# Splitting weights in two steps, separate PSUM banks and other DMA queues in an attention plus GELU feed-forward kernel

## The chip, the core and the metric

The kernel runs on one NeuronCore of one Trainium2 chip, in one launch. Its work is spread over the engines TensorE (PE in the profile; its weight loads are PEld), VectorE (DVE), ScalarE (ACT) and GpSimd (POOL); SyncE (SP) only starts DMAs. Each engine works through its own instructions in the order in which the program lists them, and waits on semaphores for the others. The metric is device time in microseconds (us); lower is better.

## What is computed

Eight batches of twelve heads go through an attention with a sigmoid in place of the softmax, and the result through a feed-forward layer with an exact GELU:

```python
scores = scale * np.matmul(q, k.transpose(0, 1, 3, 2)) - np.log(S)      # q, k, v: (8, 12, 448, 64)
attn = 1.0 / (1.0 + np.exp(-scores))
x = matmul(attn, v).transpose(0, 2, 1, 3).reshape(3584, 768)
h = x @ w_in                                                            # w_in: (768, 2048)
g = 0.5 * h * (1.0 + erf(h / sqrt(2)))
return g @ w_out                                                        # w_out: (2048, 768)
```

The weights come as 64-bit floats, so the kernel first has to decode them to fp32.

## The kernel before, in words

**Attention** takes the first quarter of the time. It walks over 24 units (8 batches x 3 groups of heads), computes scores, sigmoid and the product with v, and stores each unit's result x to a DRAM scratch `scr_x` from GpSimd's queue (`park`, L407). Beside it a `Decoder` (L99) turns chunks of 64-bit weights into fp32 on DVE and ACT and stores them to `scr_f` and `scr_out`.

**The feed-forward part** works on four blocks of two batches each. A product in full fp32 accuracy is made of three fp32r matmuls: every operand is split into a high part (a cast to fp32r, on ACT) and a low part (operand minus high part, on DVE), and `terms` (L473) issues weight-low x data-high, weight-high x data-low, weight-high x data-high, in that order. So a matmul on a tile can start only when ACT and then DVE have been at it.

Block 0 computes the first layer plainly (`ffn1_plain`, L522): 16 weight units, each used for two halves of the columns, 18 matmuls per use, 576 in all. All other layers use Winograd's variant of Strassen's scheme: seven block products in place of eight. `ffn1` (L586) does this for the first layer of blocks 1 to 3, `ffn2` (L630) for the second layer of blocks 0 to 3. Each of these seven stages is 28 weight units of 18 matmuls, 504 matmuls. The order of the products is written out by hand:

- `IN_ORDER` (L64) lists 56 products (p, j) of 9 matmuls, two to a weight unit. They run in chains: 1 then 2; 6 then 7 then 4; 5 then 3. Product p of a chain follows one step behind the one before it (`lag`), and **a chain shares one PSUM bank**: 7 is added on top of 6 in the same bank, after DVE has read the bank for 6 (L610), 4 on top of that, 3 on top of 5 (L616). After product 2 ACT applies the GELU straight from the bank; after 4, 5 and 3 DVE adds a stored sum into a `tmp` tile (L616) and ACT applies the GELU to it.
- `OUT_ORDER` (L71) lists 28 products (p, c), 18 matmuls each, block products in the order 1, 2, 5, 6, 3, 7, 4, four c each. Banks are shared in the same chains; after the fourth c ACT or DVE empties three banks (L658 to L677). Product 2 is added into product 1's banks once ACT has copied them out (L658).

The steps to be followed in the code:

- **Weights** (class `Weights`, L199). Per unit: a DMA on SP's queue into one of three staging tiles `wst` (L226), the high cast on ACT (L236) and the low part on DVE (L237) into one of four `whl` tiles. `get` for unit i first prepares up to unit i+3. Unit i+3 takes over the tile of unit i-1, so its cast waits until PE is through with that unit.
- **Operands of the second layer** (`build`, L512): high cast on ACT (L265), low part on DVE (L266), both issued two units ahead.
- **Operands of the first layer** (`x_load`, `x_sum`, `x_split`, L565 to L584): during `ffn2` of one block the x of the next is loaded (12 DMAs on SP's queue, L262, issued in unit 0), combined on DVE (L574) and split. The splits of block products 1 and 2 are issued in units 26 and 27 (L701 to L704).
- **Block sums of w_in** (`remix`, L707): loads from `scr_f` on SP's queue (L717), four DVE operations (`mix`, L93 to L96), seven or four stores to `scr_in` on GpSimd's queue (L723). j = 0 to 3 are made during `ffn2` of block 0 (units 2, 8, 14, 20, with three DRAM copies each, `recopy`), j = 4 to 7 during `ffn1` of block 1, in the tiles of g (L620).
- **x of the plain stage**: x0 (first half of the columns) is loaded and split at the end of attention (L460 to L468), x1 (second half) at the start of `ffn1_plain` (L522 to L526), six DMAs each on SP's queue.
- **PSUM**: attention has one pool of 3 x 2 banks (`ps_sc`) and one of 2 banks (`ps_av`); the feed-forward part then opens one pool of 8 banks (L744) and rotates through it.

## Time and profile before

| | us |
|---|---|
| device time, median of 3 runs | 1097.01 |
| lowest, highest | 1096.9, 1098.97 |
| the profiled execution's own time | 1101.73 |
| its span, first to last instruction | 1100.0 |
| of it attention, to the first feed-forward matmul | 259.68 |
| PE busy | 1049.5 (95% of the span) |
| DVE, ACT, POOL busy | 782.1, 603.0, 89.8 |
| granted TensorE clock, mean | 0.989 |

A row of the timeline gives start, length, engine, line of the program, operation, output <- inputs, shapes and count; the bracket at its end is the time for which that engine sat idle just before, and what ended the wait. SPq is SyncE starting DMAs. In a row of groups, "388.2, 355" is busy us and mean ns of one. Matmuls overlap: in an undisturbed stretch one starts every 0.19 us though each is listed with 0.35 us, so PE's busy share says less than the time between starts.

### The profile page before, as it was taken

How to read it: one execution, taken by the hardware profiler on the slowest of the kernel's cores; microseconds unless marked ns; L12 is line 12 of the kernel's file. 1: busy time of each engine (PE TensorE's matmuls, PEld its weight loads, DVE VectorE, ACT ScalarE, POOL GpSimd, SP SyncE). 2: the span in 40 equal slices, each digit the busy share in tenths (PEclk: the TensorE clock that was granted, in tenths of full speed). 3: DMA queues.
4: the chain of work that ended last, by engine and by line, in shares of the span. 5: the costliest groups of instructions: out<-in, count | busy, mean ns of one | idle time of the engine just before them, and what ended most of it. 6: DMA issues, size and time to landing. Idle time of an engine off the chain costs nothing.

```text
span 1100.0 us, 15452 instructions
## 1 busy us (share of the span) xinstructions
PE 1049.5 (95%) x5930; PEld 910.4 (83%) x5930; DVE 782.1 (71%) x989; ACT 603.0 (55%) x805; POOL 89.8 (8%) x142
## 2 busy tenths in 40 slices
PE   9999999997999999797998999999899999998998
PEld 5555555445999999797997899999799999988998
DVE  3777777774787688876666699566569975666795
ACT  5878877765345555354345554544455455446542
POOL 0111111002122123102000000000000000000000
PEclk9999999999999999899999999999999999999999
DMA  8999999887578777777335545433265453333442
GB/s 264 314 308 289 308 298 283 245 255 263 165 246 271 236 273 237 235 235 264 109 100 159 161 123 162 144 113 117 86 204 141 146 159 113 115 101 102 142 132 86
DMA packets 95706, 211.79 MB, mean 193 GB/s; under 512 B 9616, under 2 KB 46864, under 8 KB 95632
## 3 DMA queue, kind: packets, MB, share of 16 engines
q1 hardware_dynamic: 84560, 171.24, 51.2%
q0 software_dynamic: 10912, 39.33, 9.8%
q8 instruction: 47, 0.77, 0.3%
q10 hardware_dynamic: 160, 0.23, 0.1%
q14 instruction: 27, 0.22, 0.1%
HBM read 162.79 MB, written 50.33 MB: 194 GB/s over the span
## 4 chain that ended last, share of the span: by engine, by line
PE 75%; DVE 8%; DMA 7%; ACT 5%; issue 4%; SPq 1%; DVEq 0%; ACTq 0%
PE pf L478 53%; PE pav L386 9%; PE sc L348 8%; DVE whl L237 2%; PE sc_t L365 2%; ACT whl L236 2%; DVE tmp L616 2%; DMA wst<-scr_out 2%; PE pav L399 2%; DMA g<-scr_f 1%; DMA xl<-scr_x 1%; ACT g L504 1%; DMA wst<-scr_in 1%; DMA a<-scr_f 1%; DMA x<-scr_x 1%
## 5 line engine op out<-in xcount | busy, mean ns | idle before, releaser
L478 PE MATMUL pf<-op,whl 128*128 128x448 f32 x2016 | 388.2, 355 | 11.5 <-DVE op L266 6.8
L478 PEld LDWEIGHTS pf<-op,whl 128*128 128x128 f32 x2016 | 382.8, 190 | 16.3 <-DVE op L266 8.2
L478 PE MATMUL pf<-xh_p,whl 128*128 128x448 f32 x1008 | 280.3, 357 | 25.9 <-DVE tmp L616 16.0
L237 DVE TENSOR_TENSOR whl<-wst,whl 128x768 fp32r<-128x768 f32 x212 | 202.1, 954 | 133.6 <-ACT whl L236 133.5
L236 ACT CAST whl<-wst 128x768 fp32r<-128x768 f32 x212 | 175.8, 830 | 205.3 <-PE pf L478 166.7
L478 PEld LDWEIGHTS pf<-xh_p,whl 128*128 128x128 f32 x1008 | 192.1, 191 | 32.7 <-DVE tmp L616 18.2
L478 PE MATMUL pf<-xl_p,whl 128*128 128x448 f32 x504 | 178.9, 355 | 0.0
L331 ACT ACTIVATE a<-sc 128x896 f32<-128x896 f32 x144 | 121.7, 920 | 52.7 <-PE sc L348 52.7
L266 DVE TENSOR_TENSOR op<-g,op 128x896 fp32r<-128x896 f32 x112 | 121.2, 1084 | 9.1 <-ACT op L265 9.1
L386 PE MATMUL pav<-a,v 128*64 128x448 f32 x576 | 119.1, 548 | 0.0
L478 PE MATMUL pf<-xh,whl 128*128 128x448 f32 x384 | 105.9, 357 | 5.9 <-ACT xh L265 5.0
L265 ACT CAST op<-g 128x896 fp32r<-128x896 f32 x112 | 104.6, 935 | 2.2 <-PE pf L478 2.2
L504 ACT ACTIVATE g<-tmp 128x448 f32<-128x448 f32 x72 | 43.7, 621 | 108.9 <-DVE tmp L616 108.9
L478 PEld LDWEIGHTS pf<-xl_p,whl 128*128 128x128 f32 x504 | 96.1, 191 | 0.3
L386 PEld LDWEIGHTS pav<-a,v 128*64 128x64 f32 x576 | 37.0, 136 | 68.0 <-issue 63.6
L478 PEld LDWEIGHTS pf<-xh,whl 128*128 128x128 f32 x384 | 73.6, 192 | 7.3 <-ACT xh L265 5.3
L412 DVE COPY x<-pav 128x448 f32<-128x448 f32 x48 | 29.8, 623 | 62.6 <-PE pav L386 39.6
L478 PE MATMUL pf<-xl,whl 128*128 128x448 f32 x192 | 68.6, 357 | 1.0 <-DVE xl L266 0.8
L348 PE MATMUL sc<-lo,hi 64*128 64x448 f32 x282 | 56.9, 393 | 1.0 <-ACT a L331 1.0
L348 PEld LDWEIGHTS sc<-lo,hi 64*128 64x128 f32 x282 | 26.9, 186 | 36.7 <-ACT me L134 14.8
L131 ACT ACTIVATE me<-me 128x512 f32<-128x512 int32 (+1 forms) x40 | 29.2, 729 | 47.9 <-DVE me L120 47.9
L323 DVE TENSOR_TENSOR lo<-qk,hi 128x896 fp32r<-128x896 f32 x47 | 51.2, 1089 | 1.5 <-ACT hi L320 0.4
(76 smaller groups left out, 940.8 us busy)
## 6 DMA issues: line engine op xcount, KB each, us to landing
wst<-scr_out SPq DMA_DIRECT2D x112, 384.0 KB, 3.2
wst<-scr_in SPq DMA_DIRECT2D x84, 384.0 KB, 3.1
v<-v_dram SPq DMA_DIRECT2D x24, 512.0 KB, 5.6
raw<-w_in_dram SPq DMA_DIRECT2D x16, 768.0 KB, 7.8
raw<-w_out_dram SPq DMA_DIRECT2D x24, 512.0 KB, 5.3
scr_x<-x POOLq DMA_DIRECT2D x24, 448.0 KB, 7.1
out_dram<-tmp SPq DMA_DIRECT2D x48, 224.0 KB, 2.1
qk<-q_dram SPq DMA_DIRECT2D x23, 448.0 KB, 5.3
```

The source lines that it names most:

```text
L131: nc.scalar.activation(e.bitcast(F32), e.bitcast(I32), AF.Relu, bias=1151.0 * 2**23, scale=-8.0)
L236: nc.scalar.copy(hl[:, 0], t)
L237: nc.vector.tensor_tensor(hl[:, 1], t, hl[:, 0], op=ALU.subtract)
L265: nc.scalar.copy(hi, src)
L266: nc.vector.tensor_tensor(lo, src, hi, op=ALU.subtract)
L323: nc.vector.tensor_tensor(lo, raw, hi, op=ALU.subtract)
L331: nc.scalar.activation(to, sc, AF.Sigmoid, bias=NEG_LOG_S, scale=SCALE)
L348: nc.tensor.matmul(sc[:, j], ks[rows(j), 1, keys], braid(qs[rows(j), 0]) if braided else qs[rows(j), 0], start=n == 0, stop=n == last,)
L386: nc.tensor.matmul(pav[rows(j)], vals[u][:, p, j, c], a[:, j], start=p == 0 and c == 0, stop=p == 1 and c == FULL - 1,)
L412: nc.vector.tensor_copy(xs[u][:, p], bank(u, p))
L478: nc.tensor.matmul(bank, a, braid(m), **flags)
L504: nc.scalar.activation(straight(dst), unbraid(src), AF.Gelu)
```

## The change

- **Weights**: `prepare_to` becomes `high_to` (ACT cast) and `low_to` (DVE subtraction). `get` issues the casts up to unit i+3 but the subtractions only up to unit i+2. The staging tile is reloaded after the subtraction.
- **Second-layer operands**: `build` becomes `op_high` (two units ahead) and `op_low` (one unit ahead). First-layer operands: `x_split` becomes `x_high` and `x_low`, issued at separate products.
- **GELU and copies** of `ffn1`, and the difference of two g tiles, are put in a list `later` and issued at the start of the next product (`flush`).
- **Orders**: chains (1, 2) and (5, 3) run with lag 2; `OUT_ORDER` becomes 1, 5, 2, 6, 3, 7, 4.
- **Banks**: products 6, 7 and 4 each take banks of their own, and DVE adds the sums (7 onto g12, 4 onto g22). Products 2 and 3 stay on the banks of 1 and 5 (`CHAINED`).
- **Queues**: all loads of x and the loads of `remix` move from SP's to GpSimd's queue; an x tile takes two DMAs instead of three. `remix` becomes `mix_load` and `mix_store`, four units apart in `ffn2` and several products apart in `ffn1`. The x loads of the next block are issued in unit 1, their sums in units 16, 18, 24 and 25.
- **PSUM**: pools of 6 and 2 banks, taken in turn by the tile's number modulo 8.
- **x1 of the plain stage** is allocated and loaded before the g tiles. `LATE` goes from 18 to 17: one high cast of attention moves from ACT to DVE.

The core of the diff (lines that only rename or reflow are left out):

```diff
+        (p, s - lag * n)
+        for chain, lag in (((1, 2), 2), ((6, 7, 4), 1), ((5, 3), 2))
...
-    OUT_ORDER = [(p, c) for p in (1, 2, 5, 6, 3, 7, 4) for c in range(KF // 2)]
+    OUT_ORDER = [(p, c) for p in (1, 5, 2, 6, 3, 7, 4) for c in range(KF // 2)]
+    CHAINED = {2: 1, 3: 5}
...
-        def prepare_to(self, n):
+        def high_to(self, n):
             while self.ready < min(n, len(self.units)):
                 i = self.ready
+                self.low_to(i + 1 - WST)
                 self.load_to(i + 1)
...
                 nc.scalar.copy(hl[:, 0], t)
+                self.split[i] = hl, t
+                self.ready += 1
+
+        def low_to(self, n):
+            while self.low < min(n, len(self.units)):
+                hl, t = self.split[self.low]
                 nc.vector.tensor_tensor(hl[:, 1], t, hl[:, 0], op=ALU.subtract)
-                self.split[i] = hl
-                self.ready += 1
-                self.load_to(i + WST)
+                self.low += 1
+                self.load_to(self.low + WST)
 
         def get(self, ready=None):
             i = self.taken
-            self.prepare_to(ready or i + WHL)
+            self.high_to(ready or i + WHL)
+            self.low_to(max(i + 1, self.ready - 1))
...
-        for c in range(KC):
-            nc.sync.dma_start(dst[:, c], src[:, c, :, k])
+        for a in range(2):
+            nc.gpsimd.dma_start(dst[:, :, a], src[:, :, a])
...
             if u == total - 1:
                 for hi, lo in x0:
                     split(hi, lo, lo.bitcast(F32))
-                W.prepare_to(2)
+                W.high_to(2)
+                W.low_to(1)
             if u == total:
                 nc.scalar.activation(one, one, AF.Gelu)
-                W.prepare_to(WHL)
+                W.low_to(2)
+                W.high_to(WHL)
...
+            n = count["bank"]
+            count["bank"] += 1
+            pool = banks[n % 8 >= 6]
...
+                ph = held[CHAINED[p], j] if p in CHAINED else bank()
...
                 if p == 1:
-                    nc.scalar.copy(g21, ph)
+                    later.append(lambda g21=g21, ph=ph: nc.scalar.copy(g21, ph))
                 elif p == 2:
-                    gelu(g11, ph)
+                    later.append(lambda g11=g11, ph=ph: gelu(g11, ph))
                 elif p == 6:
-                    nc.vector.tensor_tensor(g12, ph, g21, op=add)
+                    combine(g12, ph, g21, add)
                 elif p == 7:
-                    nc.vector.tensor_tensor(g22, ph, g21, op=add)
+                    combine(g22, ph, g12, add)
...
+                    def close(p=p, r=r, h=h, dst=dst, t1=g[0, 1][c], g11=g[0, 0][c]):
+                        gelu(dst, h)
+                        if p == 3 and r == 1:
+                            later.append(lambda: combine(t1, t1, g11))
+                    later.append(close)
+                at = p, j
+                if b == 1 and at in ((1, 3), (1, 4), (1, 7), (2, 6)):
+                    jm = 4 + ((1, 3), (1, 4), (1, 7), (2, 6)).index(at)
+                    mix_store(jm)
+                    if jm < 6:
+                        mix_load(jm + 2, g)
+                highs = {(1, 2): 6, (1, 5): 7, (1, 7): 4, (6, 3): 5, (7, 7): 3}
+                lows = {(1, 3): 6, (1, 6): 7, (2, 6): 4, (6, 4): 5, (4, 7): 3}
...
             for n, (p, c) in enumerate(OUT_ORDER):
                 hl = W.get()
-                build(b, g, n + 2)
+                op_high(b, g, n + 2)
+                op_low(n + 1)
+                flush()
...
-                if b == 0 and n % 6 == 2 and n // 6 < KF // 2:
-                    remix(n // 6)
-                    recopy(n // 6 + KF // 2)
+                if b == 0:
+                    if n % 6 == 0 and n // 6 < KF // 2:
+                        mix_load(n // 6)
+                        recopy(n // 6 + KF // 2)
+                    if n % 6 == 4 and n // 6 < KF // 2:
+                        mix_store(n // 6)
...
                     if (p, c) == (4, 2):
-                        x_split(nxt, b + 1, 1)
+                        x_high(nxt, b + 1, 1)
                     if (p, c) == (4, 3):
-                        x_split(nxt, b + 1, 2)
+                        x_low(nxt, 1)
+                        x_high(nxt, b + 1, 2)
...
-    ps_f = ctx.enter_context(psum("ps_f", 8))
-    feed_forward(ps_f)
+    banks = [ctx.enter_context(psum(f"ps_f{n}", n)) for n in (6, 2)]
+    feed_forward(banks)
```

In the new `ffn2` the lines shown last stand behind the loop over the three banks of the product, as the old ones did. `x_low(xs, 2)` is issued at product 0 of the next `ffn1`.

More of the change, by code (lines that the diff above doesn't have):

```diff
@@ L206, in __init__ @@
             self.staged, self.split = {}, {}
-            self.loaded = self.ready = self.taken = 0
+            self.loaded = self.ready = self.low = self.taken = 0
         def source(self, i):
@@ L478, in terms, with feed_forward, flush @@
             nc.tensor.matmul(bank, a, braid(m), **flags)
-    def feed_forward(ps_f):
-        ff = late
+    def feed_forward(banks):
         sub, add = ALU.subtract, ALU.add
-        count = [0]
+        count = {"bank": 0, "tmp": 0}
+        later = []
         def bank():
-            count[0] += 1
-            return ps_f.tile([P, 512], F32, tag="pf", name=f"pf{count[0]}")[:, :S]
+            n = count["bank"]
+            count["bank"] += 1
+            pool = banks[n % 8 >= 6]
+            return pool.tile([P, 512], F32, tag="pf", name=f"pf{n}")[:, :S]
         def tmp():
-            count[0] += 1
-            return ff.tile([P, S], F32, tag="tmp", name=f"tmp{count[0]}", bufs=4)
+            count["tmp"] += 1
+            return late.tile([P, S], F32, tag="tmp", name=f"tmp{count['tmp']}", bufs=4)
+        def flush():
+            now = later[:]
+            later.clear()
+            for work in now:
+                work()
         def slots(b):
@@ L550, in ffn1_plain @@
                 if f == 0:
-                    dec.pool = ff
+                    dec.pool = late
                     dec.flush()
@@ L592, in ffn1 @@
                     hl = W.get()
-                key = chain_of[p], j
-                first = p in (1, 6, 5)
-                if first:
-                    banks[key] = bank()
-                ph = banks[key]
-                hi, lo = ops[p]
+                flush()
+                if n == 0:
+                    x_low(xs, 2)
+                ph = held[CHAINED[p], j] if p in CHAINED else bank()
+                held[p, j] = ph
+                hi, lo = xs[p]
                 for cc in range(KC):
@@ L637, in ffn2 @@
             p1, p5, u2 = (x_tile(f"xt{n}", f"y{b}_{n}").bitcast(F32) for n in range(3))
-            chains = {1: "a", 2: "a", 5: "c", 3: "c", 6: "b", 7: "b", 4: "b"}
-            banks = {}
-            nxt, x = {}, {}
+            held, nxt, x = {}, {}, {}
             for n, (p, c) in enumerate(OUT_ORDER):
                 hl = W.get()
-                build(b, g, n + 2)
-                if c == 0 and p in (1, 5, 6):
-                    banks[chains[p]] = [bank() for _ in range(KE)]
-                bs = banks[chains[p]]
-                op = built.pop(n)
+                op_high(b, g, n + 2)
+                op_low(n + 1)
+                flush()
+                if c == 0:
+                    fresh = p not in CHAINED
+                    held[p] = [bank() for _ in range(KE)] if fresh else held[CHAINED[p]]
+                op = ops.pop(n)[0]
                 for e in range(KE):
+                    ph = held[p][e]
                     for f in range(2):
@@ L652, in ffn2 @@
                         o = op[:, 0, f * S : f * S + S], op[:, 1, f * S : f * S + S]
-                        first = p in (1, 5, 6) and c == 0 and f == 0
-                        last = c == KF // 2 - 1 and f == 1
-                        terms(bs[e], w, o, first, last, True)
+                        ends = fresh and c == 0 and f == 0, c == KF // 2 - 1 and f == 1
+                        terms(ph, w, o, *ends, True)
                     if c == KF // 2 - 1:
                         if p == 1:
-                            nc.scalar.copy(p1[:, e], bs[e])
+                            nc.scalar.copy(p1[:, e], ph)
@@ L659, in ffn2 @@
                         elif p == 5:
[L660 removed]
+                            nc.scalar.copy(p5[:, e], ph)
                         elif p == 6:
[L662 to L666 removed]
+                            combine(u2[:, e], ph, p1[:, e], add)
@@ L713, in remix, with mix_store @@
                 a = sb.tile([P, 4 * QUAD], F32, tag="wd", name=f"a{j}", bufs=2)
-                t = ff.tile([P, 4 * QUAD], F32, tag="s", name=f"sin{j}", bufs=1)
+                t = late.tile([P, 4 * QUAD], F32, tag="s", name=f"sin{j}", bufs=1)
                 tiles = [x[:, i * WU : i * WU + WU] for x in (a, t) for i in range(2)]
             for i in range(2):
-                nc.sync.dma_start(tiles[i], scr_f[i * KF + j])
-            quads = [t[:, i * OP : i * OP + OP] for t in tiles for i in range(2)]
+                nc.gpsimd.dma_start(tiles[i], scr_f[i * KF + j])
+            mixes[j] = [t[:, i * OP : i * OP + OP] for t in tiles for i in range(2)]
+        def mix_store(j):
+            quads = mixes.pop(j)
             parts = mix(quads[:4], quads[4:])
             for p, part in parts.items():
-                if not (g and p in (1, 2, 4)):
+                if j < KF // 2 or p not in (1, 2, 4):
                     n = IN_ORDER.index((p, j))
```

210 lines of the change are left out of this document (105 added, 105 removed).

## The prediction

> **What bounds the kernel now.** I read the page first, then the stretches of the feed-forward part by stage, then what PE waited for, then the timeline around each wait. The page's first line gives the span, and the view of stretches the eight stages (first the plain first layer of block 0, then second and first layers in turn):
>
> ```profile
> span 1100.0 us, 15452 instructions
> ...
> 259.68:377.43 117.75, 111.82 (x577) 110.12 (x577) 83.20 (x130) 49.37 (x82) 31.08 (x43) 0.97 0.73 237
> 377.43:482.70 105.27, 98.46 (x506) 96.51 (x504) 88.05 (x102) 53.04 (x67) 21.32 (x40) 0.97 0.75 248
> 482.70:593.95 111.25, 98.83 (x506) 95.92 (x506) 68.24 (x93) 49.92 (x73) 8.54 (x16) 0.98 0.50 162
> 593.95:694.34 100.39, 97.59 (x506) 96.29 (x505) 82.93 (x90) 52.84 (x68) 0.00 (x0) 0.98 0.52 159
> 694.34:799.23 104.89, 98.14 (x505) 95.95 (x504) 62.03 (x78) 50.62 (x73) 0.00 (x0) 0.98 0.38 112
> 799.23:896.86 97.63, 95.90 (x505) 94.93 (x505) 81.55 (x89) 52.60 (x67) 0.00 (x0) 1.00 0.54 163
> 896.86:1000.31 103.45, 96.68 (x506) 94.78 (x506) 60.56 (x77) 50.30 (x73) 0.00 (x0) 1.00 0.37 114
> 1000.31:1096.24 95.93, 95.79 (x505) 94.83 (x503) 73.28 (x82) 48.22 (x63) 0.00 (x0) 1.00 0.41 119
> ```
>
> The columns are: stretch, length, busy time (and count) of PE, PEld, DVE, ACT and POOL, granted clock, DMA share, GB/s. The last seven stages do the same 504 matmuls, yet take from 95.93 to 111.25 us. The last one has next to no idle time, so 95.93 is the floor of such a stage (3.43 per unit of 18 matmuls, 0.19 per matmul), and 576/504 x 95.93 = 109.6 that of the plain one. Over the floor are, in order, 8.1, 9.3, 15.3, 4.5, 9.0, 1.7, 7.5 and 0: 55.4 us. TensorE's stream is the bound, and these are holes in it. What ended the holes:
>
> ```profile
> PE pf L478 <- DVE tmp L616: 16.0, 12, 3.2
> PE pf L478 <- DVE op L266: 6.8, 4, 4.9
> PE pf L478 <- DVE g L610: 6.1, 3, 3.2
> PE pf L478 <- ACT xh L265: 5.0, 1, 5.0
> PE pf L478 <- ACT y L658: 4.3, 2, 2.7
> PE pf L478 <- DVE whl L237: 3.7, 1, 3.7
> ...
> PE pf L478 <- DVE x L412: 1.0, 1, 1.0
> ...
> DVE whl L237 <- ACT whl L236: 133.5, 107, 5.1
> ```
>
> PE's waits make 42.9 us; the rest of the 55.4 is mostly matmuls that run at half rate after a long hole (listed with 0.74 us below). The last row is behind many of them: DVE, in order, stands 133.5 us idle before weight subtractions whose cast ACT has not done, with its other work queued behind.
>
> **Where each hole comes from.** From the timeline:
>
> ```profile
> 458.24 0.56 DVE L93 TENSOR_TENSOR sin<-a 128x384 f32<-128x384 f32 x1 [3.72 <-DMA a<-scr_f]
> 463.73 0.74 PE L478 MATMUL pf<-op,whl 128*128 128x448 f32 x1 [4.94 <-DVE op L266]
> 500.30 0.56 DVE L93 TENSOR_TENSOR g<-g 128x384 f32<-128x384 f32 x1 [4.19 <-DMA g<-scr_f]
> 795.28 0.62 DVE L616 TENSOR_TENSOR tmp<-pf,g 128x448 f32<-128x448 f32 x1
> 795.96 0.74 PE L478 MATMUL pf<-xh_p,whl 128*128 128x448 f32 x1 [3.23 <-DVE tmp L616]
> 799.76 6.60 SPq L262 DMA_DIRECT2D x<-scr_x  x12
> 812.46 0.83 ACT L236 CAST whl<-wst 128x768 fp32r<-128x768 f32 x1 [4.49 <-DMA wst<-scr_out]
> 814.61 1.59 PE L478 MATMUL pf<-op,whl 128*128 128x448 f32 x7 [1.59 <-ACT y L658]
> ```
>
> Second layer of block 0: DVE waits for a block load that has just been started, and the operand splits stand behind it. The change starts that load four units (13.7 us) ahead and on another queue. First layer of block 1: the same with loads into g (500.30), and weight loads behind them on SP. First layers of blocks 1 to 3: PE may not add the next product into a shared bank until DVE has read it (795.28, 795.96); DVE is late because it waits for a GELU in ACT's queue. The change gives 6, 7 and 4 banks of their own, leaves four products between 5 and 3 and runs the GELU a product later, so none of these reads is near PE's path. Second layers of blocks 1 and 2: twelve x loads occupy SP for 6.6 us, the next weight unit comes late (812.46), and product 2 waits for ACT to empty product 1's banks (814.61). With x on GpSimd's queue and all four units of product 5 in between, both go. So I take these holes away and ask what is late next.
>
> **What is late next: the block edge.** In the new order the low part of x for product 1 is issued in unit 27 behind the three additions that empty product 4's banks. Before, it was issued a unit earlier, and only product 2's stood there:
>
> ```profile
> 482.70 0.35 PE L478 MATMUL pf<-xh_p,whl 128*128 128x448 f32 x1
> ...
> 482.90 0.62 DVE L670 TENSOR_TENSOR tmp<-pf,y 128x448 f32<-128x448 f32 x1 [0.51 <-PE pf L478]
> 483.44 1.55 DVE L266 TENSOR_TENSOR xl_p<-x,xh_p 128x1344 fp32r<-128x1344 f32 x1
> ```
>
> The last addition can start only 0.2 us after the stage's last matmul, the subtraction 0.54 later, and it takes 1.55: ready 2.3 us into the new stage. The second matmul of the stage needs it and would start at 0.19. New hole: 2.1, taken as 2.2, at the start of each of three first layers.
>
> **What is late next: after product 6.** The operand's low part now has a lead of one unit, not two. DVE operations follow each other at these distances, with the longer ones beside them:
>
> ```profile
> 438.49 1.08 DVE L684 TENSOR_TENSOR g<-g,g 128x896 f32<-128x896 f32 x1
> 439.49 0.95 DVE L237 TENSOR_TENSOR whl<-wst,whl 128x768 fp32r<-128x768 f32 x1
> 440.36 1.08 DVE L266 TENSOR_TENSOR op<-g,op 128x896 fp32r<-128x896 f32 x1
> ...
> 406.94 1.56 DVE L574 TENSOR_TENSOR x<-x,x 128x1344 f32<-128x1344 f32 x1
> ...
> L93 DVE TENSOR_TENSOR sin<-a 128x384 f32<-128x384 f32 x4 | 2.2, 560 | 8.5 <-DMA a<-scr_f 8.5
> ```
>
> An ordinary unit with a g difference takes DVE 1.00 + 0.87 + 1.00 = 2.9 of 3.43: it can run ahead. The end of product 6 ties it to PE: last addition at 0.20, +0.54, g difference +1.00, weight +0.87, operand +1.08 = 3.7 us after the product's end, needed at 3.43: a hole of 0.3 in each second layer. In block 0, the same unit (16) then holds a block mix (4 x 0.56 = 2.2) and an x sum (1.5), before the next weight (0.87) and operand (1.08): 3.6 + 2.2 + 1.5 + 0.87 + 1.08 = 9.3, needed at 0.3 + 2 x 3.43 = 7.2: 2.1 more. So 2.5 there. Elsewhere the same walk ends in time (after product 7, six additions of 0.55: 3.3 against 3.43).
>
> **The start.** The first feed-forward matmul waits for DVE's copy out of the last attention bank, and x1 is late:
>
> ```profile
> 252.00:260.00 8.00, 7.01 (x40) 2.34 (x37) 6.83 (x8) 6.56 (x8) 0.89 (x2) 1.00 0.31 105
> 260.00:268.00 8.00, 8.00 (x44) 7.99 (x43) 3.85 (x6) 1.92 (x3) 6.15 (x9) 1.00 1.00 329
> ...
> 259.68 0.43 PE L478 MATMUL pf<-xh,whl 128*128 128x448 f32 x1 [0.99 <-DVE x L412]
> ...
> 266.15 11.26 DMA xl<-scr_x
> ...
> 275.09 0.74 PE L478 MATMUL pf<-xh,whl 128*128 128x448 f32 x1 [4.96 <-ACT xh L265]
> ...
> 277.51 1.31 ACT L265 CAST xh<-xl 128x1344 fp32r<-128x1344 f32 x1 [2.48 <-DMA xl<-scr_x]
> ...
> L168 POOL DMA_DIRECT2D scr_out<-s x24 | 17.3, 753 | 57.0 <-DVE s L93 52.5 <-DVE s L96 1.9 <-PE pf L478 1.7
> ```
>
> With a pool of its own the last two banks of attention no longer hold up the first matmul: -1.0. Bounds: if the x0 loads, which now stand behind an x store on GpSimd's queue, came late, the first matmul could be up to 2 us later than before; the DMA share of 0.31 in the stretch before says that the backlog is gone by then, so I take the gain. x1: four starts of 0.75 from 260.5 on, ahead of the `scr_out` stores, which contended with them. Ahead or beside them lie the last x store (448 KB) and two weight units (768 KB); with x1's 1344 KB that is 2.6 MB, at 329 GB/s 8.0 us: landed near 268.5, cast (1.31) and subtraction (1.55) done by 271.4. PE needs this half at 258.7 + 3 x 3.43 + 9 x 0.19 = 270.7. A hole of 0.7, taken as 1.5; bounds 0 (loads alone on the queue) and the present 8.1.
>
> [...]
>
> **Sum.** Over the floor after the change, by stage: 1.5, 2.5, 2.5 (2.2 and 0.3 for block loads), 0.3, 2.2, 0.3, 2.2, 0.3 = 11.8 against 55.4; with the first gap 43.6 + 1.0 = 44.6 us less. The 48 starts that move to GpSimd (24 for the later x, 8 for x0 and x1, 16 for the blocks; 0.75 each, 36 us) lie on an engine with 0 to 31 us of work per stage. A block load there waits until the stores of the mix before have left its tile, and DRAM copies and, in unit 0, the x loads queue behind it; their first users come four units later or more, so I cost that at 0.3 in the first layer of block 1 alone. The one cast that moves from ACT to DVE in attention (`LATE`) I take at nothing, bounds 1 us either way. The profiled execution took 1101.7, so 1057.1 of its kind; it lies 4.7 above the median of the three timed runs, and from that median, 1097.0, I get 1052.4. No hole at all would be 1097.0 - 56.4 = 1040.6.
>
> **Rivals.** First: the data come late all the same. Speaks for it that DMA moves 329 GB/s at a share of 1.00 at the start and 0.75 in block 0; against it, that weight loads no longer stand behind other loads on SP and have about two units to land. Price: the plain stage keeps 8.1 and the first layer of block 1 its 15.3: 1052.4 + 6.6 + 12.8 = 1071.8.
>
> Second: GpSimd is held up by DVE. If it could start DMAs only while DVE is idle, 0.75 becomes 0.75 / (1 - 83.20/117.75) = 2.6 and x1 lands 7.3 later: 1059.7. The later x loads have 15 units, 51 us, before their first use and would hide it.
>
> Third, slower than before: DVE becomes the bound of the second layers because the operand's low part has one unit less of lead. If every unit waited as long for a cast as DVE's weight subtractions do now (133.5 / 107 = 1.25 us), then with 82.93 / 28 = 2.96 us of work it takes 4.21 against 3.43: 0.78 x 112 units = 87 us, 3.4 of which I have already, 1136 in all. It turns the sign from 0.4 us per unit on, that is a wait of 0.87. Against it: each of these subtractions follows its cast by a whole unit in the new order.
>
> Fourth: the banks bring nothing. Tile number modulo 8 over pools of 6 and 2 is the same rotation as one pool of 8, so except for the first gap that part does nothing; if the other moves only shifted the holes, no change. Fifth: the block edge costs nothing (the subtraction runs earlier than I read): 6.6 less, 1045.8.
>
> **How the numbers follow.** My forecast 0.62, the fifth case 0.11, the first rival 0.15, the second 0.06, the third 0.04, no change 0.02. Faster by over 0.2% (2.2 us, about what a measurement of this kernel can tell from no change): 0.94; within: 0.02; slower: 0.04. The range goes from 1044, which holds the fifth case, to 1068, which takes in the second rival and a partial first one; the full first, the third and no change stay out.
>
> **What would show it.** Right: the seven stages of 504 matmuls lie between 96 and 99 us; PE no longer waits for L616, L610 or L658's counterparts; DVE's waits for the weight cast all but vanish from 133.5; the second matmul of each first layer of blocks 1 to 3 waits about 2 us for a low part of x; one hole near unit 17 of block 0's second layer. Wrong: first matmul later than 259.7, x1 landing after 271, a hole in most units of a second layer (third rival), or the first layer of block 1 still above 105 us.

## The result, and the profile after

The changed kernel takes 1058.37 us (median, 1056.78 to 1059.09), the kernel before 1097.49 in the runs beside it (1096.9 to 1098.97): a ratio of 0.964, 95% interval 0.9623 to 0.9656. The forecast was 1052.4 with a range of 1044 to 1068: the sign is right, the range holds the time, and the median lies 6.0 us above the forecast.

Two lines of the page after the change (the profiled execution's own time is 1057.68):

```profile
span 1055.8 us, 15495 instructions
...
PE 1038.8 (98%) x5930; PEld 907.9 (86%) x5930; DVE 785.4 (74%) x990; ACT 605.4 (57%) x804; POOL 122.8 (12%) x190
```

DVE and ACT are as busy as before (782.1 and 603.0); their work was only moved. POOL has 33.0 us more: the 48 DMA starts that came over from SP, 0.54 to 0.78 each.

The view of stretches after the change, in the same eight stages and with the same columns as before:

```profile
259.18:372.97 113.79, 111.28 (x576) 110.25 (x577) 85.00 (x133) 51.49 (x85) 41.58 (x59) 0.99 0.80 260
372.97:470.54 97.57, 95.91 (x505) 94.92 (x505) 84.93 (x100) 51.67 (x67) 26.39 (x49) 1.00 0.78 265
470.54:568.14 97.60, 95.61 (x505) 95.17 (x505) 71.51 (x96) 52.58 (x75) 16.76 (x28) 1.00 0.62 198
568.14:663.78 95.64, 95.64 (x505) 95.07 (x505) 80.73 (x88) 52.21 (x66) 0.00 (x0) 1.00 0.49 141
663.78:761.38 97.60, 95.61 (x505) 95.17 (x505) 63.85 (x79) 51.58 (x74) 6.06 (x8) 1.00 0.48 146
761.38:857.02 95.64, 95.64 (x505) 95.06 (x505) 80.74 (x88) 52.32 (x66) 0.00 (x0) 1.00 0.48 141
857.02:956.31 99.29, 97.30 (x506) 96.54 (x506) 63.85 (x79) 51.78 (x74) 0.00 (x0) 0.98 0.38 116
956.31:1052.11 95.80, 95.80 (x505) 94.91 (x503) 73.41 (x82) 47.49 (x61) 0.00 (x0) 1.00 0.42 122
```

The seven stages of 504 matmuls, which took 95.93 to 111.25 us, now take 95.64 to 99.29. Stage for stage, the time over the floor of 95.93 (109.6 in the plain stage) as forecast and as found:

| stage | before | forecast | after |
|---|---|---|---|
| plain, block 0 | 8.1 | 1.5 | 4.2 |
| second layer, block 0 | 9.3 | 2.5 | 1.6 |
| first layer, block 1 | 15.3 | 2.5 | 1.7 |
| second layer, block 1 | 4.5 | 0.3 | -0.3 |
| first layer, block 2 | 9.0 | 2.2 | 1.7 |
| second layer, block 2 | 1.7 | 0.3 | -0.3 |
| first layer, block 3 | 7.5 | 2.2 | 3.4 |
| second layer, block 3 | 0 | 0.3 | -0.1 |
| sum | 55.4 | 11.8 | 11.8 |

(The last sum is of unrounded figures; the stages after add up to 792.93.)

What PE waited for in the feed-forward part, where there had been 42.9 us of waits, and DVE's wait for the cast of the weights (133.5 before), from the view of waits. In each row: waiting engine, tile and line, what it waited for, us in all, times, longest:

```profile
PE pf L488 <- DVE xl_p L525: 6.0, 3, 2.0
PE pf L488 <- DVE op L525: 1.7, 1, 1.7
...
PE pf L488 <- ACT xh L273: 1.4, 1, 1.4
PE pf L488 <- DVE xl L274: 1.1, 1, 1.1
...
DVE whl L245 <- ACT whl L238: 64.7, 58, 5.9
```

The old rows (`tmp`, `g` and `y`, the reads of shared banks) are gone. Five rows are left in this part. Four were named ahead: the block edge (`xl_p`) three times, unit 17 to 18 of block 0 once (`op`), and x1, cast and low part (`xh`, `xl`). The fifth, 0.3 for the first unit's weights (`whl`), is told at the start below. The block edge in the timeline of the changed kernel:

```profile
469.47 1.90 DVE L525 TENSOR_TENSOR tmp<-pf,y 128x448 f32<-128x448 f32 x3
...
470.54 0.35 PE L488 MATMUL pf<-xh_p,whl 128*128 128x448 f32 x1
471.29 1.55 DVE L525 TENSOR_TENSOR xl_p<-x,xh_p 128x1344 fp32r<-128x1344 f32 x1
...
472.89 0.46 PE L488 MATMUL pf<-xl_p,whl 128*128 128x448 f32 x1 [1.99 <-DVE xl_p L525]
```

Three additions into `tmp`, then the subtraction (`xl_p`) 0.75 after the stage's first matmul, 1.55 long; the second matmul starts 2.35 after the first in place of 0.19. That is 2.16 lost, against 2.2 forecast.

The start in the same timeline. At 244.69 the x0 loads are started behind an x store on POOL's queue, and both casts of x0 wait for them:

```profile
243.97 0.72 POOL L423 DMA_DIRECT2D scr_x<-x  x1 [9.55 <-DVE x L420]
244.69 3.17 POOL L270 DMA_DIRECT2D xl<-scr_x  x4
...
253.42 1.31 ACT L273 CAST xh<-xl 128x1344 fp32r<-128x1344 f32 x1 [0.79 <-DMA xl<-scr_x]
...
255.36 1.31 ACT L273 CAST xh<-xl 128x1344 fp32r<-128x1344 f32 x1 [0.63 <-DMA xl<-scr_x]
...
256.37 2.48 PE L394 MATMUL pav<-a,v 128*64 128x448 f32 x12
...
259.18 0.46 PE L488 MATMUL pf<-xh,whl 128*128 128x448 f32 x1 [0.34 <-DVE whl L245]
...
261.37 3.04 POOL L270 DMA_DIRECT2D xl<-scr_x  x4
...
271.23 1.31 ACT L273 CAST xh<-xl 128x1344 fp32r<-128x1344 f32 x1 [0.25 <-DMA xl<-scr_x]
```

The wait for the last attention bank is gone (before: 0.99, `DVE x L412`), but the weights of the first unit, which DVE splits behind x0, are 0.34 late. Of x1, started at 261.37, the last half is there only at about 271.2 (its cast, at 271.23, has just waited 0.25 for it).

### The profile page after: what moved, and what is told of

Read it like the earlier page. It is cut to its first block, busy times and chain, and to the rows that moved or that the text cites. A ratio compares the mean times of both kernels' runs of the same rounds, so it can differ in the third digit from the quotient of the medians.

```text
span 1055.8 us, 15495 instructions
## 1 busy us (share of the span) xinstructions
PE 1038.8 (98%) x5930; PEld 907.9 (86%) x5930; DVE 785.4 (74%) x990; ACT 605.4 (57%) x804; POOL 122.8 (12%) x190
## 3 DMA queue, kind: packets, MB, share of 16 engines
q0 software_dynamic: 15264, 56.64, 15.3%
## 4 chain that ended last, share of the span: by engine, by line
PE 93%; DVE 2%; DMA 2%; issue 2%; ACT 1%; POOL 0%; DVEq 0%; POOLq 0%; ACTq 0%
PE pf L488 71%; PE pav L394 10%; PE sc L356 8%; PE sc_t L373 2%; PE pav L407 2%; DMA wst<-scr_out 1%; DMA xl<-scr_x 1%; DVE xl_p L525 0%; DMA qk<-k_dram 0%; DVE op L525 0%; POOL xl L270 0%; DVE g L525 0%; DVE whl L245 0%; DVE wd L146 0%; ACT a L339 0%
## 5 line engine op out<-in xcount | busy, mean ns | idle before, releaser
L488 PE MATMUL pf<-op,whl 128*128 128x448 f32 x2016 | 383.5, 353 | 1.7 <-DVE op L525 1.7
L488 PE MATMUL pf<-xh_p,whl 128*128 128x448 f32 x1008 | 274.7, 354 | 0.0
L245 DVE TENSOR_TENSOR whl<-wst,whl 128x768 fp32r<-128x768 f32 x212 | 201.9, 953 | 64.8 <-ACT whl L238 64.7
L525 DVE TENSOR_TENSOR g<-g,g 128x896 f32<-128x896 f32 x64 | 69.3, 1083 | 0.0
L525 DVE TENSOR_TENSOR tmp<-pf,g 128x448 f32<-128x448 f32 x72 | 44.7, 624 | 27.4 <-PE pf L488 25.6
L522 ACT ACTIVATE g<-tmp 128x448 f32<-128x448 f32 x72 | 45.2, 627 | 33.4 <-DVE tmp L525 33.3
L525 DVE TENSOR_TENSOR g<-pf,g 128x448 f32<-128x448 f32 x48 | 29.9, 624 | 37.5 <-PE pf L488 36.4
```

The source lines that it names most:

```text
L245: nc.vector.tensor_tensor(hl[:, 1], t, hl[:, 0], op=ALU.subtract)
L488: nc.tensor.matmul(bank, a, braid(m), **flags)
L522: nc.scalar.activation(straight(dst), unbraid(src), AF.Gelu)
L525: nc.vector.tensor_tensor(out, a, b, op=op)
```

## The experiments

Line numbers in the rows are those of each experiment's own kernel. Three theories. **Causes apart** is the prediction's: each hole has its own cause, and what removes it is one named part. **Casts**: DVE standing in front of weight subtractions is the one cause; the weights part does nearly everything. **Overlap**: a hole needs two late things, so that parts don't add up.

The kernel before is not steady: beside the runs below its median is 1097.5 (parts undone), 1101.1 (parts alone) and 1098.3 (holes that are left), with single executions from 1094.58 to 1103.81. So differences between these groups are known to some 4 us only, and the stages of a profile say more than the totals.

### One part of the changed kernel undone

**Weights** (the low part follows its cast at once again):

```diff
                 self.split[i] = hl, t
                 self.ready += 1
+                self.low_to(self.ready)
```

> The changed kernel, but with the low part of each weight unit issued right behind its high cast again. Three theories. 'Causes apart' (the prediction's): every hole has a cause of its own; here only block 0's second layer, where DVE has block mixes to catch up with, loses some: 1059 to 1063, DVE's idle time before weight subtractions back from 65 to 120 us or more. 'Casts': the one cause of nearly all holes is that DVE stands behind casts that ACT hasn't done; then this undoing brings most of them back: 1078 or more. 'Overlap': a hole needs two things to be late at once, so that undoing any one part costs little: 1058 to 1061.

1075.39 us (1074.44 to 1078.17), ratio 0.9802 (0.9785 to 0.9819): 17.0 more than the changed kernel. From the view of waits:

```profile
PE pf L489 <- DVE op L526: 14.9, 13, 3.2
PE pf L489 <- DVE xl_p L526: 7.6, 3, 3.6
...
DVE whl L246 <- ACT whl L238: 155.3, 148, 5.8
```

The second layer of block 0 has 11.1 of it (97.57 to 108.62), no other stage more than 3.3. DVE stands behind casts 155.3 us again, and what is late on its queue is the operand's low part, which in the new order is issued only one unit ahead. So the split of the weights is what makes the short lead of the operands affordable. The time lies in none of the three ranges expected, nearest to that of "casts"; but the first layers of blocks 2 and 3 stay at 97.60 and 99.28, which "casts" does not explain.

**Queues** (x and block loads back on SP's queue):

```diff
-            nc.gpsimd.dma_start(dst[:, :, a], src[:, :, a])
+            nc.sync.dma_start(dst[:, :, a], src[:, :, a])
...
-                nc.gpsimd.dma_start(tiles[i], scr_f[i * KF + j])
+                nc.sync.dma_start(tiles[i], scr_f[i * KF + j])
```

> The changed kernel, but with the loads of x and of the weight blocks on SyncE's queue again. 'Causes apart': the holes that followed from weight loads standing behind other loads come back at the start (about 4 us), in the second layer of block 0 and the first of block 1 (3 to 6 us each), and 1 or 2 us in the second layers of blocks 1 and 2: 1066 to 1074. 'Casts': at most 3 us more, 1061. 'Overlap': 3 to 8 us more, most of it at the start: 1061 to 1066.

1062.91 us (1062.51 to 1063.96), ratio 0.9685 (0.9671 to 0.97): 4.5 more. The plain stage is longer by 5.3, 119.06 against 113.79; PE's wait for x1's cast grows from 1.4 to 5.3 us. Block loads, x of the later blocks and weights share SP's queue here and no other stage is longer by more than 1.7 (block 2's first layer, where the clock is at 0.50 for 3.4 us behind the block edge). The time lies in the range of "overlap". With `remix` split in two, loads and mix units apart, the queue of the block loads does not matter here.

**Banks** (7 and 4 back in the bank of 6, in both layers, with their sums; the chains 1, 2 and 5, 3 back to a lag of one):

```diff
-        for chain, lag in (((1, 2), 2), ((6, 7, 4), 1), ((5, 3), 2))
+        for chain, lag in (((1, 2), 1), ((6, 7, 4), 1), ((5, 3), 1))
...
-    CHAINED = {2: 1, 3: 5}
+    CHAINED = {2: 1, 3: 5, 7: 6, 4: 7}
```

> The changed kernel, but with block products 6, 7 and 4 in one bank again and a lag of one step in all chains (the sums that DVE adds go back with it). 'Causes apart': the holes of the first layers of blocks 1 to 3 at shared banks come back, 5 to 7 us in each: 1073 to 1079. 'Casts': at most 1061, since DVE now reads the banks in time. 'Overlap': 1 or 2 us in each first layer: 1061 to 1065.

1060.36 us (1059.01 to 1063.03), ratio 0.9664 (0.9647 to 0.9681): 2.0 more, in first layers (100.93, 99.24, 99.24 us); PE waits for the copy of g on ACT three times, 2.6 us in all. Of block 1's 100.93, 1.7 are half-rate matmuls (the clock is at 0.50 from 472.0 to 475.4). "Causes apart" expected 1073 to 1079 and misses by far; "casts" had at most 1061, "overlap" 1061 to 1065.

**GELU** (the list `later` runs at once):

```diff
-        later = []
+        class Now(list):
+            def append(self, work):
+                work()
+
+        later = Now()
```

> The changed kernel, but with the GELU, the copies and the g differences of the first layers issued at once and not at the next product. 'Causes apart': DVE waits for a GELU before each g difference again, but with four products between 5 and 3 that reaches PE only at the end of the chain: 2 to 8 us more, 1060 to 1066. 'Casts' and 'overlap': no more than 2 us, 1058 to 1060.

1058.85 us (1056.37 to 1061.14), ratio 0.9654 (0.9638 to 0.967): 0.5 more, no difference that these runs can show. The second layers of blocks 1 to 3 take 1.35 more each, so the part does something, about 4 us in the profiled execution. There it is made up elsewhere: the start is 1.7 earlier, the plain stage 2.07 shorter (111.72), and block 3's first layer is at 97.60 like the other two, for the clock stays at 1.00 behind its edge. "Causes apart" had expected a loss in the first layers; there is none.

The four add up to 24.0 us, the whole change is worth 39.1. That alone says little, since the four are not the whole change: the order of the second layer's products, the pools of PSUM, `remix` in two steps and the later operand low parts stay in all of them, and no run undoes these. What each part brings alone decides.

### One part alone on the kernel before

**Weights** alone, the split of the change's `high_to` and `low_to` without the rest:

```diff
-            self.prepare_to(ready or i + WHL)
+            self.high_to(ready or i + WHL)
+            self.low_to(max(i + 1, self.ready - 1))
```

> The kernel before, with one part of the change alone: weight units' low parts issued a unit behind their casts. 'Casts': with the one cause gone most of the 39 us are gained, 1062 to 1077. 'Causes apart': 8 to 15 less than before, 1082 to 1089, since shared banks, block loads on SyncE's queue and product 1's copy stay. 'Overlap': each part alone gains more than undoing it costs; for this one, whose undoing cost 17 us: 20 or more, up to 1077.

1128.93 us (1126.37 to 1130.66) against 1101.12 beside it (1094.58 to 1103.81): ratio 1.0253 (1.0209 to 1.0298), 27.8 **slower**. All three theories expected a gain. "Casts" as the one cause falls: DVE's wait for casts of weights goes from 133.5 to 9.6 us, and the kernel loses. ACT's waits say where:

```profile
ACT whl L237 <- DMA wst<-scr_out: 82.3, 23, 10.0
ACT whl L237 <- DMA wst<-scr_in: 33.3, 5, 9.8
```

In the kernel before these two were 17.5 and 10.1. The staging tile is free only after the low part, and the low part comes a unit later; the next weight load starts later by as much. Where x and block loads stand on the same queue, it is late. First layers of blocks 2 and 3, where nothing else is loaded, gain: 97.22 and 97.23 in place of 104.89 and 103.45. The shared queue and three tiles are not enough for the loss, though: the changed kernel with its loads back on SP's queue has both, and there ACT waits 25.3 us for `wst<-scr_out`, not 82.3. Which of the other parts spares it is not shown.

**The same with a fourth staging tile:**

```diff
-WHL, WST = 4, 3
+WHL, WST = 4, 4
```

> The weights part alone on the kernel before, as in the run that came out 27.8 us slower, with a fourth staging tile. If that loss is lost lead (the tile is freed by the low part, which now comes a unit later, so a weight load starts 3.4 us later and more often stands behind x or block loads on SP's queue), a fourth tile gives the lead back: second layers of blocks 0 to 2 back to 98 to 107 us, first layer of block 1 to 111 or less, ACT's waits for the weight load from 82 + 33 us to under 35, total 1070 to 1090 against 1097 to 1101 for the kernel before. If it is DVE (low parts of weights in the way of its other work), it stays near 1125 to 1129.

1103.64 us (1099.08 to 1107.88), ratio 1.0043 (1.0024 to 1.0063): it lies 5.3 above the kernel before where the run without the tile lay 27.8 above, so lost lead was most of that. ACT's waits for weight loads fall from 82.3 and 33.3 to 11.6 (the row of `scr_in` is gone), but DVE has another one:

```profile
ACT whl L237 <- DMA wst<-scr_out: 11.6, 3, 4.9
...
DVE g L93 <- DMA g<-scr_f: 29.4, 4, 8.8
```

The stretches of the first layer of block 1 and the second layer after it:

```profile
487.13:611.88 124.75, 103.43 (x506) 100.17 (x504) 68.30 (x93) 50.71 (x73) 8.54 (x16) 0.92 0.45 143
611.88:709.24 97.36, 96.16 (x505) 94.93 (x505) 82.78 (x90) 52.86 (x68) 0.00 (x0) 1.00 0.56 166
```

The time expected was missed all the same (1070 to 1090): the second layers of blocks 1 and 2 came back (97.36 and 97.33), block 0's only to 110.87 (98 to 107 expected), and the first layer of block 1 not at all (124.75; 111 or less expected). There DVE waits 29.4 us for block loads into g (11.5 before), with the weights' low parts behind it. The timeline shows a ring:

```profile
490.35 0.34 SPq L226 DMA_DIRECT2D wst<-scr_in  x1
490.74 0.90 SPq L727 DMA_DIRECT2D g<-scr_f  x2
495.71 0.56 DVE L93 TENSOR_TENSOR g<-g 128x384 f32<-128x384 f32 x1 [5.42 <-DMA g<-scr_f]
...
497.72 0.95 DVE L244 TENSOR_TENSOR whl<-wst,whl 128x768 fp32r<-128x768 f32 x1
498.69 0.32 SPq L226 DMA_DIRECT2D wst<-scr_in  x1
499.05 0.92 SPq L727 DMA_DIRECT2D g<-scr_f  x2
```

DVE's mix waits for the block load; the next weight low part stands behind the mix; the next weight load waits for that low part to free its staging tile; and the next block load stands behind that weight load on SP's queue. It goes round once per block, some 10 us each. With loads and mix some products apart the hole is not there, whichever queue the loads take (97.60 in the changed kernel and in the run with SP's queue); no run takes `remix` apart alone.

**Banks** alone (in the first layers only, the lags too; the sums of 7 and 4 move to DVE as in the change):

```diff
-                first = p in (1, 6, 5)
+                first = p in (1, 6, 7, 4, 5)
...
-                    nc.vector.tensor_tensor(g22, ph, g21, op=add)
+                    nc.vector.tensor_tensor(g22, ph, g12, op=add)
```

> The kernel before, with own banks for block products 6, 7 and 4 in the first layers and a lag of two steps in the chains 1, 2 and 5, 3, alone. 'Casts': at most 8 us less than before, 1089 or more. 'Causes apart': the holes of the first layers of blocks 2 and 3 (9.0 and 7.5 us over the floor) and about half of block 1's go: 18 to 24 less, 1073 to 1079. 'Overlap': as 'causes apart', though undoing this part cost 2 us only.

1089.86 us (1085.12 to 1092.85), ratio 0.9897 (0.9853 to 0.9942): about 11 less. First layers of blocks 2 and 3 go to 97.49 and 97.48, block 1's to 103.68: 21 us in all. That is what "causes apart" and "overlap" had expected (18 to 24), but their total, 1073 to 1079, is missed, for second layers lose some of it: block 1's takes 103.82 (100.39 before) and block 2's 103.98 (97.63 before), with PE waiting 3.1 and 3.4 us for ACT to empty product 1's banks and the clock at 0.50 for 6.8 us in each.

**Queues** alone (`remix` stays in one piece, and an x tile keeps its three DMAs):

```diff
-            nc.sync.dma_start(dst[:, c], src[:, c, :, k])
+            nc.gpsimd.dma_start(dst[:, c], src[:, c, :, k])
...
-                nc.sync.dma_start(tiles[i], scr_f[i * KF + j])
+                nc.gpsimd.dma_start(tiles[i], scr_f[i * KF + j])
```

> The kernel before, with the loads of x and of the weight blocks on GpSimd's queue, alone (each block load still directly ahead of its mix). 'Casts': at most 5 us less, 1092 or more. 'Causes apart': about 4 us each at the start, in block 1's first layer and together in the second layers of blocks 1 and 2; in block 0's second layer DVE still waits for the load: 10 to 15 less, 1082 to 1087. 'Overlap': 5 to 15 less.

1100.14 us (1098.11 to 1102.11), ratio 1.0003 (0.9981 to 1.0025). The plain stage gains 6.7 (111.09) and the second layers of blocks 0 to 2 2.9, 4.1 and 0.9; the first layer of block 1 loses 14.3 (125.58), and the gap ahead of the first feed-forward matmul grows from 1.53 to 2.90. In block 1 it is ACT that waits for weights, whose blocks come out of `remix` (10.1 before):

```profile
ACT whl L236 <- DMA wst<-scr_in: 31.4, 6, 11.2
```

The timeline says why these come later. On GpSimd's queue each block load stands behind the four stores of the block before (478.50 and 480.64, then 489.73 and 491.87, 501.00 and 503.14), and those wait for DVE's mix, so loading and mixing take turns: DVE waits 24.4 us for block loads in place of 11.5, and the last block's stores start 39.4 us into the stage. In the kernel before it is 25.9: there SP started two of the four loads ahead of the first stores (484.49 and 486.25; 492.24).

**GELU** alone (GELU, copies and differences of g one product later):

```diff
-                    gelu(g11, ph)
+                    later.append(lambda g11=g11, ph=ph: gelu(g11, ph))
```

> The kernel before, with the GELU, the copies and the g differences of the first layers issued at the next product, alone. 'Casts': no more than 5 us less. 'Causes apart': the holes at the end of chain 5, 3 follow from a g difference that waits for a GELU ahead of the read of a shared bank; these (about 5 us in each of three first layers) go: 10 to 15 less, 1082 to 1087. 'Overlap': as 'causes apart', though undoing this part cost nothing.

1073.87 us (1071.86 to 1075.89), ratio 0.9756 (0.972 to 0.9792): 27 less, the most of any part and twice what was expected. The first layer of block 2 in the view of stretches:

```profile
685.07:780.41 95.34, 95.34 (x505) 95.18 (x505) 61.05 (x77) 50.88 (x73) 0.00 (x0) 1.00 0.41 124
```

95.34 us, and as much in block 3: under what had been taken as the floor, although the banks are still shared.

In the first layers of blocks 2 and 3, then, most of the hole goes with any one of three parts: weights (97.2), banks (97.5) or GELU (95.3). That is overlap: DVE's read of a shared bank was late because of casts **and** of the GELU, and it mattered only because the bank was shared. This is why taking back banks or GELU alone costs 2.0 and 0.5, while each alone brings 11 and 27. Causes apart would have a part bring alone what it costs to undo: as a rule for sharing out the gain it falls.

### The holes that are left

**Block edge** (x's high part for product 1 a unit earlier, its low part ahead of the additions of product 4):

```diff
+                    if (p, c) == (4, 1):
+                        x_high(nxt, b + 1, 1)
                     if (p, c) == (4, 2):
-                        x_high(nxt, b + 1, 1)
-                    if (p, c) == (4, 3):
                         x_low(nxt, 1)
+                    if (p, c) == (4, 3):
                         x_high(nxt, b + 1, 2)
```

> The changed kernel with one thing moved: the copy and the subtraction that split x for product 1 are issued one unit earlier, so that the subtraction no longer stands behind the additions that empty product 4's banks. Causes apart, and the prediction's block edge: the three holes of 2.16 us at the second matmul of a first layer (and the 1.7 us of half-rate matmuls behind one of them) go, nothing else is late, so 6.5 to 8.2 us less than 1058.4: 1050 to 1052, first layers of blocks 1 to 3 at 95.4 us each. Overlap: something else stands just behind the subtraction (the x copy on ACT, the weight unit of unit 26), and half or less of it comes back: 1054 to 1057.

1047.46 us (1047.15 to 1048.51) against 1098.33 beside it (1096.32 to 1101.89), ratio 0.9528 (0.95 to 0.9556): 10.9 less than the changed kernel, and 2.5 under the lower end expected. The timeline at the first edge:

```profile
464.99 1.55 DVE L525 TENSOR_TENSOR xl_p<-x,xh_p 128x1344 fp32r<-128x1344 f32 x1
...
468.57 0.35 PE L488 MATMUL pf<-xh_p,whl 128*128 128x448 f32 x1
...
468.76 0.35 PE L488 MATMUL pf<-xl_p,whl 128*128 128x448 f32 x1
```

The first layer of block 1 in the view of stretches:

```profile
468.57:563.91 95.34, 95.34 (x505) 95.26 (x505) 70.31 (x95) 52.00 (x75) 16.75 (x28) 1.00 0.63 203
```

The subtraction is done 2.0 us before the stage begins, the second matmul follows the first at 0.19, and all three first layers take 95.34: 2.26, 2.26 and 3.95 less by the profiles, 8.5 in all. The block edge is a cause by itself, as causes apart had it. The other 2.0 of the spans' difference of 10.4 lie ahead of the first place that the edit touches: the first feed-forward matmul is at 257.56 in this execution (259.18 in that of the changed kernel), and the plain stage is 0.35 shorter. What moves the end of attention from one execution to the next stays open. No other version here is faster.

**Three more holes at once**: x0 on SP's queue, the operand's low part ahead of product 6's additions, and an x sum one unit later.

```diff
-                    load_x(x0[j][1], 0, j, 0)
+                    load_x(x0[j][1], 0, j, 0, nc.sync)
...
                 op_low(n + 1)
+                if (p, c) == (6, KF // 2 - 1):
+                    op_low(n + 2)
...
-                    if (p, c) == (3, 0):
+                    if (p, c) == (3, 1):
                         nxt[5] = x_sum("xt3", b + 1, 5, x[0, 1], x[0, 0])
```

> The same, and three more of the holes that are left: the x loads for product 1 in its first half back on SP's queue, the operand's low part for the unit after the last of product 6 issued ahead of the additions that empty its banks, one x sum of block 1 to 3 moved from unit 16 to unit 17 so that it no longer follows a block mix. Causes apart: block edges -6.5 to -8.2, unit 17 to 18 of block 0 -1.8, four times -0.16 after product 6, the start -1 to -3: 1045 to 1049. Overlap: the holes at unit 17 and after product 6 only move by a unit and the start is bound by the landing of x: 1050 to 1053.

1048.04 us (1046.8 to 1049.26), ratio 0.953 (0.9505 to 0.9555): no better than the run before it (it lies in the range of "causes apart" only because that run was already better than expected). The second layers of blocks 1 to 3 gain 0.26 each (95.38, 95.37 and 95.54), and the first feed-forward matmul follows attention's last one at 0.47 without a wait, against 0.83 to 0.87 with x0 on GpSimd. But block 0's second layer loses 1.65 (99.22). DVE's rows around product 6's end:

```profile
425.33 1.09 DVE L525 TENSOR_TENSOR op<-g,op 128x896 fp32r<-128x896 f32 x1 [1.00 <-ACT op L537]
426.33 1.68 DVE L525 TENSOR_TENSOR y<-pf,y 128x448 f32<-128x448 f32 x3
...
432.66 1.08 DVE L525 TENSOR_TENSOR op<-g,op 128x896 fp32r<-128x896 f32 x1
```

The low part moved ahead now waits 1.00 us for its own cast on ACT, so the three additions begin 56.1 us into the stage in place of 53.6 (426.55 in the changed kernel), the block mix and the rest follow, and PE again waits 1.9 us for the operand of unit 18. So the two holes have only moved into one, as "overlap" had it: PE loses 2.05 at unit 18 in place of 0.26 after product 6 and 1.83 at unit 18. The 1.65 are not its size but what follows it: the clock is at 0.50 from 434.59 to 438.00, which it was not in the changed kernel.

**The kernel before, profiled again:**

> The kernel before, profiled once more. Its profile lay 4.2 to 4.7 us above its timed median, that of the changed kernel 0.7 below. If the first profile of the kernel before was an unlucky one of a spread that timed runs have too (1095 to 1104), this span lies between 1093 and 1098, and one or two stages that wait for loads are shorter; if profiling itself costs this kernel 4 us, it is 1099 to 1101 again with the same stages.

1098.7 us, span 1096.8. One row differs by much from the first profile, the second layer of block 1 (100.39 there):

```profile
592.55:689.65 97.10, 95.90 (x505) 94.94 (x505) 81.49 (x89) 52.62 (x67) 0.00 (x0) 1.00 0.54 164
```

The first feed-forward matmul is at 258.10 in place of 259.68. The other stages are within 1.4 us, of both signs, and the eight together take 835.00 in place of 836.56. Part of this is the clock: in block 1's second layer it was at 0.50 for 3.4 us (from 611.24) in the first profile and never in the second, in block 3's second layer the other way round (from 995.12). So profiling does not by itself cost this kernel 4 us: this profile lies 0.4 above the median of the runs beside it, the first one lay 4.7 above.

## Why the prediction was right, and where its sizes were off

**The bound and the holes.** Right. The stages are 95.6 to 99.3 us (96 to 99 was the sign named), and no wait on a shared bank is left. The reason given for the first layers (DVE late behind a GELU in ACT's queue) holds: that part alone takes these stages of blocks 2 and 3 to 95.34. It is not the only one, since weights or banks alone take away most of the hole too. For the second layers of blocks 1 and 2 the prediction named two remedies, x on GpSimd's queue and product 5 in between. The queue is not needed: with x back on SP's queue they stay at 95.64 and 95.63, though alone it brings 4.1 and 0.9. The new order was not tried alone.

**Block edge.** Right in place and size: 2.16 for 2.2, three times, and the run without it gets it back. The 0.3 for block loads in block 1 does not show: its first layer takes 97.60 as block 2's does.

**After product 6, unit 17 to 18.** Right in place. 0.26 for 0.3 after product 6 (0.16 and 0.10 at two matmuls), and 1.83 for 2.1 in block 0: the walk along DVE's distances was good to 0.3 us. The table's second layers lie under the floor because 95.93 itself held some idle time; the undisturbed stage is 95.34.

**First gap.** -1.0 forecast. From attention's last matmul to the first of the feed-forward part it was 1.53 before and is 0.87: -0.66. The DMA share of 0.31 had been read as "the backlog is gone"; both casts of x0 waited for their loads all the same. The bound named there was the right one, x0 behind a store on POOL's queue. With x0 on SP's queue the gap is 0.47, the whole 1.0.

**x1.** The term that was sized wrong: 1.5 forecast, 4.2 found in the plain stage. It was started at 261.37 for 260.5, and the last half was there at 271.2 for 268.5, past the 271 that the prediction gave as a sign of being wrong. Besides, the walk took only the last half. PE asks for the first half at its fourth unit's first matmul (271.03 less the 1.53 lost, 269.5), 9 matmuls earlier, and its cast starts only at 269.67, after a wait of 2.83 for the load; both of PE's waits are for this half. PE loses 1.53 and 1.40 there, and most of the other 1.3 in matmuls 0.37 apart, at half rate, until 276.7 (granted clock 0.52 from 273.3 on).

**First layer of block 3.** 3.4 for 2.2: the same hole, and behind it 1.7 us of half-rate matmuls (granted clock 0.51 from 860.2 to 863.5) that the other two edges did not have.

**The sum** of the stages came out as forecast (11.8), and that is luck: these two errors, 2.7 and 1.2 too little, are made up by the other six stages, which are 0.4 to 0.9 under their forecast. By the profiled execution's own time it is 1057.68 for 1057.1.

**The transfer to the median** is where the 6.0 us come from. The holes were those of one execution, at 1101.73; they were taken off a median 4.7 lower, as if an execution at the median held the same ones. The profile after lies 0.7 under its own median, and the sum itself was 0.6 too hopeful: 4.7 + 0.7 + 0.6 = 6.0. Which holes the median execution lacks stays open. The second profile of before, at 1098.7, starts 1.6 earlier and has 53.9 over the floor in place of 55.4: block 1's second layer has 3.3 less, but other stages have more. With its 53.9, 43.0 would have come off in place of 44.6 and the forecast would have been 1054.0, still 4.4 short. The base itself is uncertain by as much: medians of the kernel before go from 1097.0 to 1101.1.

**DVE's wait for weight casts** did not all but vanish: 64.7 us are left of 133.5. It cost PE 0.3, because what stands behind it now has time to spare.

**Rivals.** Data late anyway: seen for x1 alone, at 2.7 over forecast, not for block 1 (1.7). The reason given against it does not hold as it stands: ACT waits as long for weight loads as before (16.9, 13.1 and 1.9 us from `scr_out`, `scr_in` and `scr_f`; 17.5, 10.1 and 2.1 before). That the loads land earlier is not shown; what is shown is that PE no longer feels the wait. GpSimd held up by DVE: not seen. The row of groups for the later x loads, which are started in second layers with DVE busy 80.73 to 84.93 us of each:

```profile
L270 POOL DMA_DIRECT2D x<-scr_x x24 | 18.2, 761 | 229.4 <-DVE xl_p L525 225.8 <-PE pf L488 3.7
```

761 ns per start, as ahead of the change (753). DVE as the bound of second layers: not in the change, but 11.1 us of it in block 0's as soon as the weights' low part follows its cast at once. No change from banks: they bring 11 alone, and 2 on top of the rest.

## What to carry to other kernels

Splitting a producer into two steps on two engines takes a step's wait out of the second engine's queue (DVE's wait for casts of weights went from 133.5 to 9.6 us in the weights part alone), but the buffer between them is held longer (there ACT's wait for `wst<-scr_out` went from 17.5 to 82.3). Look whether the load behind it can still start in time; where it could not (the weights part alone), one buffer more gave back most of the loss, while the changed kernel did without it. Parts that shorten the same hole do not add up, so a part's worth is a number only together with what else is in place. Before a sum of holes is taken off a median, the holes should come from an execution that is itself near that median, or from several profiles, whose spread is then the least that the forecast can be off by.

## What the runs showed of the hardware

Two holes of the same length had different aftermaths. At 666.13 and 859.37 of the changed kernel PE had been idle for 1.99 and 2.00 us, at the second and third block edge. The rows of the timeline:

```profile
666.13 0.46 PE L488 MATMUL pf<-xl_p,whl 128*128 128x448 f32 x1 [1.99 <-DVE xl_p L525]
...
859.37 0.46 PE L488 MATMUL pf<-xl_p,whl 128*128 128x448 f32 x1 [2.00 <-DVE xl_p L525]
```

The view of stretches for the four microseconds after each:

```profile
859.40:863.40 4.00, 4.00 (x13) 3.71 (x14) 3.12 (x3) 0.53 (x1) 0.00 (x0) 0.61 0.35 104
666.20:670.20 4.00, 4.00 (x21) 4.00 (x22) 3.08 (x3) 1.09 (x2) 3.00 (x4) 1.00 0.54 135
```

The granted clock was 0.61 behind the third edge and 1.00 behind the second (and behind the first), with 13 matmuls against 21: 1.7 us of further loss (99.29 against 97.60 for the stage), or none. What decides it is not shown here; two executions of one kernel differ in it (the second layer of block 3 in the two profiles of before, at 1.00 and 0.99). In the slow stretch here matmuls are 0.37 apart from 860.2 to 863.5, at a granted clock of 0.51; behind the second edge they are 0.19 apart.
